# A recurrence and a gated feed-forward block on one core: second weight loads tied to other rows, and a new late order

## Chip, cores and metric

The kernel runs on one core of one Trainium2 chip. The metric is device time in microseconds (us) of the whole program, as the median of several runs. Engines: PE is TensorE, DVE VectorE, ACT ScalarE, POOL GpSimd, SP SyncE (which here only issues transfers). PEld is the weight load of TensorE, listed apart from its matmuls.

## What is computed

Inputs r, k, v, w have the shape (batch 4, heads 8, time 768, 48), u is (8, 48), all float32. The feed-forward weights are w_in (384 x 1024), conv_w (3 x 1024) and w_out (1024 x 384). They arrive as float64, which the kernel reads as pairs of 32-bit words. Cut to its core:

```python
for t in range(S):                       # per batch and head, state is 48 x 48
    cur = u * k[t] (outer) v[t]
    y[t] = r[t] @ (state + cur)
    state = w[t][:, None] * state + k[t] (outer) v[t]
x = y as (4, 768, 384)                   # the 8 heads side by side
h = relu(x @ w_in)                       # 384 -> 1024
conv = conv_w[0]*h[t-1] + conv_w[1]*h[t] + conv_w[2]*h[t+1]
out = (h * sigmoid(conv)) @ w_out        # 1024 -> 384
```

## The kernel before

**Tiling.** The 768 time steps of a batch are cut into 6 chunks of 128, so there are N = 24 chunks; chunk n works on all 8 heads at once. The feed-forward runs on 8 blocks of 384 time steps, two per batch. Blocks 6 and 7 are the last batch's. Chunk 21 is that batch's fourth chunk; block 6 needs its rows.

**A chunk.** `loads` (L653, SP) fetch w, k, r, v. PE turns them (L685), a scan on DVE makes the decay products in `kr`. Six small transfers on SP (`spread`, L728, 16 partitions each) bring pieces of `kr` into `last`, so that all heads stand where the matmuls want them. PE then makes the scores of the chunk, `half` (L843 on `kr` and `last`, and `fresh`, L853, on v and `kh`, a copy of k turned back by L752), and for the chunk before it `output`: L811 carries the old state in, L821 adds what comes from within the chunk. DVE makes the new state: `sa` (L886), `s` (L893), `sd` (L779), and ACT adds one part of `sd` from `last` (L782). An `output` lies in two PSUM banks. ACT copies its high half into xT (L903) and DVE the rest (L905). Six more small transfers on SP (L914) spread the heads that did not fit. After that xT holds the rows x of the feed-forward.

**A block.** Per feature slice of 128 (8 of them) PE makes 9 products x @ w_in (L925: three parts of 128 rows, times three for the high and low halves). The gating of a slice is a chain: relu (ACT L937), scale (ACT L938), two sums (DVE L939, L941), sigmoid (ACT L943), product (DVE L944), cast (ACT L946) and rest (POOL L947). Three products x w_out per slice and 128 time steps (L954) add up in one bank per 128 time steps. The sum is copied into `wide` (ACT L993) and sent (SP L994); the last block's banks are copied half on DVE (L988), half on ACT (L987) and sent from ACT's queue (L990).

**Word checks.** The weights were turned from float64 at the start. Whether all words were in the range that this way of reading them covers is checked late: `again(k)`, k = 0 to 5, loads the raw words a second time from ACT's queue (L640). The first three loads are a third of w_in, 1 MB each; the next two are three transfers of 384 KB of w_out, the last is two of them. Each goes into a slot of the ring `gh`, which it shares with the gated results. Two ACT passes per load (L570) add what is out of range into `flags`; PE sums the flags (L1108), and at the end a branch takes the program `general` if a flag is set. It isn't here.

**What sets the order.** Nothing of the order is written out by hand. Each step is given to a planner, `Plan`, with its reads, its writes and a rank. The planner simulates the engines with fixed lengths and takes the ready step with the lowest rank. The rank is the chunk's or block's own plus SHIFT[stage], SHIFT[kind] and FINE["stage.op"], which are tables of numbers; the stages are l, a, b (loads and two halves of a chunk), i, o (in- and out-products of a block), q (the second loads) and k. What comes out is one list per engine, which that engine goes through in order. On the chip a step waits only for the data and the buffers that it uses, and for what stands ahead of it in its engine's list. So a read that is given to the planner alone, such as the reads of `again`'s loads, puts the load behind something in the list, but makes no wait by itself.

**Transfers.** All transfers of SP and ACT take eight completion semaphores in turn, DMAHW0 to DMAHW7, in the order in which the program is built. An issue waits until the transfer that had this turn before it has landed.

Of the kernel before, what the change touches and what calls it, by code (L numbers as in the profile page):

```python
# [52 lines left out]
    a1=486, a10=10, a11=-18, a12=1721, a13=-81, a14=373, a15=1550, a16=-5, a17=-3444, a18=228, a19=55, a2=-187,  # L53
    a20=-277, a21=143, a22=-588, a23=-345, a3=564, a4=-460, a5=2857, a6=-907, a7=26, a8=-1139, adg=2121, adsel=469,
    afill=-1128, agather=278, aguard=-10, akback=101, akh=236, akt=-56, aones=259, ascan=8, asmall=202, aspread=80,
    atop=1, atr=6061, az=192, azh=-1916, b0=293, b1=54, b10=172, b11=311, b12=-289, b13=205, b14=-397, b16=-43,
    b17=-811, b18=422, b19=19, b2=8, b20=-700, b21=-277, b22=-4, b23=-23, b24=557, b3=-36, b4=114, b5=-77, b6=179,
    b8=-463, b9=123, bcph=2596, bcross=123, bhalf=477, boutput=378, bs=3878, bsa=-378, bsd=-16, bsdl=365, bsmall=10,
    bspread=-21, bxhih=-35, bxloh=-4306, c=-10, cexp=97, cfill=-99, cissue=-266, clo=239, ctr=191, cwords=-316,
    cwstt=-125, cwts=-21, i0=-310, i2=438, i3=-28, i5=-794, i6=-2808, i7=147, icast=-1967, igate=-1561, imm3=3579,  # L60
    imul=-1362, irelu=285, isig=-154, istt=1127, k=302, kissue=225, ksmall=-331, l0=-133, l1=55, l11=147, l12=-694,
    l13=-381, l14=143, l16=-1142, l17=-179, l18=361, l19=-27, l2=-167, l20=1421, l21=35, l22=-499, l23=-90, l3=-175,
    l4=-219, l5=-37, l7=19, l8=-366, l9=146, lload=5054, o0=-231, o1=195, o2=-305, o3=135, o4=-155, o5=-163, o6=966,
    o7=186, oissue=-72, omm3=8366, oout=-13, p0=-400, p1=-1988, p10=-778, p11=-1950, p12=-115, p13=-232, p14=-285,
    p15=589, p16=-556, p2=16, p3=-496, p4=5592, p5=162, p6=315, p7=29, p9=125, pcast=963, pexp=-965, plo=-954,
    pwstt=1024, pwts=1129, q0=1176, q2=-364, q3=1730, q4=-120, q5=166, qissue=-174, qwords=273, w1=-800, w2=105,
# [339 lines left out]
def rwkv_conv_moe_kernel(  # L406
# [13 lines left out]
    B, H, S, D = r.shape  # L420
# [9 lines left out]
    KT = DM // P  # L430
# [196 lines left out]
    def again(k):  # L627
# [10 lines left out]
        def fetch():  # L638
            for a, c in parts:
                nc.scalar.dma_start(out=a(), in_=c)  # L640
        op("ACT", "issue" if k < KT else "sends", fetch, [chunks[N - 1][x] for x in "wkrv"] + [("flag", N + 2 * k - 1)] * (k >= 1), [(raw, 0)],
           [raw], moves=(0.0027 * n, 309.0 if k < KT else 122.0, 8))
        small_words(words, raw, k, n, [(raw, 0)])

# [503 lines left out]
```

## Time and profile before

| | |
|---|---|
| time, median of 3 runs | 341.63 us (341.41 to 343.01) |
| the profiled execution | 342.61 us; its span in the trace 340.9 us; mean granted clock of TensorE 0.97 |
| busy of the span | PE 93%, PEld 87%, DVE 77%, ACT 65%, POOL 54% |
| moved | 41.36 MB, 121 GB/s in the mean |

A row of the timeline or the chain starts with its start in us from the start of the span and its length; brackets at its end give how long the engine stood idle before it and what ended that. ACTq and SPq are the engines' transfer issues. A row of windows lists, per stretch, the busy time of PE, PEld, DVE, ACT and POOL with the number of instructions, then the granted clock (1.00 is full), the mean busy share of the 16 DMA engines, and GB/s. A row of groups has busy us and mean ns of one, then the idle time ahead.

### The profile page before, as it was taken

To read this page: it belongs to the slowest core of one execution; us is meant where nothing else is said; L and a number is where in the kernel's file an instruction comes from. 1 tells how busy PE (TensorE), PEld (TensorE's weight loads), DVE (VectorE), ACT (ScalarE), POOL (GpSimd) and SP (SyncE) were. 2 spreads that over 40 slices of the span, in tenths; PEclk is the share of its full clock that TensorE was granted. 3 is DMA by queue.
4 is the path that set the end of the run, shared out by engine and by line. 5 is a ranking of instruction groups with operands and counts; after the bars stand their busy time and mean duration, and the time that the engine had idled before them with its cause. 6 is when DMAs were issued, how large, how long until landed. Compare 5 with 4: busy or idle time off the path is not lost.

```text
span 340.9 us, 11483 instructions
## 1 busy us (share of the span) xinstructions
PE 315.7 (93%) x4510; PEld 295.6 (87%) x4510; DVE 264.0 (77%) x623; ACT 222.9 (65%) x587; POOL 184.3 (54%) x242
## 2 busy tenths in 40 slices
PE   7858858789999999999999999999999989999993
PEld 3746647689999999989999999999999979999993
DVE  5899978899999798699887976899997526575340
ACT  4266435896886752578876534787954758898760
POOL 8978974898584862156862731438543501343140
PEclk9989995799999999999999999999999999999998
DMA  8997764661552374268152634564416445304212
GB/s 164 326 344 144 209 167 94 127 120 38 107 120 58 87 144 101 46 136 176 34 128 64 135 65 100 115 138 105 106 27 173 139 105 171 138 23 163 92 47 77
DMA packets 114546, 41.36 MB, mean 121 GB/s; under 512 B 103197, under 2 KB 110902, under 8 KB 113718
## 3 DMA queue, kind: packets, MB, share of 16 engines
q1 hardware_dynamic: 112036, 30.55, 40.6%
q10 hardware_dynamic: 2018, 6.88, 6.1%
q0 software_dynamic: 432, 3.15, 2.3%
q8 instruction: 36, 0.59, 0.7%
q14 instruction: 24, 0.20, 0.2%
HBM read 31.48 MB, written 4.72 MB: 106 GB/s over the span
## 4 chain that ended last, share of the span: by engine, by line
PE 73%; DMA 8%; DVE 7%; POOL 6%; issue 2%; ACT 2%; SPq 1%; POOLq 0%; DVEq 0%; ACTq 0%
PE bank L925 30%; PE bank L954 27%; PE bank L685 5%; PE bank L811 3%; DMA gh<-in_moe_w_in_dram,limits 3%; PE bank L821 2%; PE bank L843 2%; DMA last<-kr 2%; DMA gh<-in_moe_w_out_dram 2%; PE bank L853 2%; PE bank L752 2%; DMA k<-in_k_dram 1%; DVE wide L561 1%; POOL wo L579 1%; DVE kr L694 1%
## 5 line engine op out<-in xcount | busy, mean ns | idle before, releaser
L947 POOL TENSOR_TENSOR gh<-g,gh 128x384 fp32r<-128x384 f32 x64 | 64.8, 1020 | 98.5 <-ACT gh L946 97.2
L954 PE MATMUL bank<-wo,gh 128*128 128x384 f32 x576 | 117.5, 345 | 0.0
L925 PE MATMUL bank<-xT,wi 128*128 128x386 f32 x576 | 112.1, 347 | 1.5 <-issue 0.7
L925 PEld LDWEIGHTS bank<-xT,wi 128*128 128x128 f32 x576 | 104.0, 193 | 2.6 <-DVE dA L699 1.1
L954 PEld LDWEIGHTS bank<-wo,gh 128*128 128x128 f32 x576 | 98.8, 188 | 0.8
L939 DVE SCALAR_TENSOR_TENSOR a<-bank,cw,a 128x384 f32<-128x384 f32 x64 | 39.0, 611 | 19.0 <-ACT a L938 18.5
L937 ACT ACTIVATE bank<-bank 128x386 f32<-128x386 f32 x64 | 30.6, 478 | 22.1 <-PE bank L925 20.8
L944 DVE TENSOR_TENSOR g<-bank,a 128x384 f32<-128x384 f32 x64 | 35.1, 550 | 12.7 <-POOL gh L947 7.7
L744 POOL TENSOR_SCALAR_AFFINE_SELECT pm<-dg 64x512 f32<-64x512 f32 x46 | 30.2, 657 | 19.1 <-PE bank L821 14.0
L941 DVE SCALAR_TENSOR_TENSOR a<-bank,cw,a 128x384 f32<-128x384 f32 x64 | 38.9, 609 | 1.4 <-DVE a L939 0.4
L938 ACT ACTIVATE a<-bank,cw 128x384 f32<-128x384 f32 x64 | 37.0, 580 | 4.2 <-DVE g L944 2.4
L946 ACT CAST gh<-g 128x384 fp32r<-128x384 f32 x64 | 32.1, 510 | 10.5 <-DVE g L944 8.2
L943 ACT ACTIVATE a<-a 128x384 f32<-128x384 f32 x64 | 33.5, 523 | 5.7 <-DVE a L941 5.1
L732 POOL TENSOR_TENSOR z<-r,k 128x384 f32<-128x384 f32 x24 | 24.3, 1012 | 14.9 <-DVE dg L735 8.4
L694 DVE TENSOR_TENSOR_SCAN kr<-bank,one_end 128x387 f32<-128x387 f32 x24 | 22.9, 954 | 4.7 <-POOL kr L516 2.7
L903 ACT CAST xT<-bank 112x256 fp32r<-112x256 f32 x48 | 16.0, 377 | 14.4 <-PE bank L821 14.3
L734 POOL TENSOR_TENSOR z<-z,ubc 128x384 f32<-128x384 f32 x24 | 24.3, 1012 | 1.1
L811 PE MATMUL bank<-kr,sa 48*64 48x64 f32 (+1 forms) x288 | 21.0, 231 | 2.7 <-DVE bank L868 1.1
L702 DVE TENSOR_TENSOR_SCAN kr<-bank,dA 128x387 f32<-128x387 f32 x24 | 22.9, 952 | 0.1
L811 PEld LDWEIGHTS bank<-kr,sa 48*64 48x64 f32 (+1 forms) x288 | 14.6, 128 | 8.4 <-issue 3.1
L564 POOL TENSOR_TENSOR wide<-wide,wide 128x384 int32<-128x384 int32 (+2 forms) x18 | 16.7, 930 | 7.7 <-DVE wide L561 6.5
L905 DVE TENSOR_TENSOR xT<-bank,xT 112x256 fp32r<-112x256 f32 x48 | 18.2, 412 | 3.1 <-ACT xT L903 2.9
(108 smaller groups left out, 547.8 us busy)
## 6 DMA issues: line engine op xcount, KB each, us to landing
w<-in_w_dram SPq DMA_DIRECT2D x24, 192.0 KB, 3.9
k<-in_k_dram SPq DMA_DIRECT2D x24, 192.0 KB, 3.0
r<-in_r_dram SPq DMA_DIRECT2D x24, 192.0 KB, 3.4
v<-in_v_dram SPq DMA_DIRECT2D x24, 192.0 KB, 3.4
out_dram<-wide SPq DMA_DIRECT2D x21, 192.0 KB, 2.8
gh<-in_moe_w_in_dram ACTq DMA_DIRECT2D x3, 1024.0 KB
gh<-in_moe_w_out_dram ACTq DMA_DIRECT2D x8, 384.0 KB, 3.8
gh<-in_moe_w_out_dram SPq DMA_DIRECT2D x2, 1152.0 KB, 10.0
```

The lines of the kernel that those rows point to most:

```text
L744: op("POOL", "zh", lambda p=slice(HL * j, HL * (j + 1)): nc.gpsimd.affine_select(out=pm.t[p].rearrange("p g m t -> p (g m) t"), in_=dg.t[p ...
L811: nc.tensor.matmul(to(h, m, c, w), lhsT=q["sa" if h else "sd"].t[p, m, 0:w], rhs=rt(out_of, m)[p, HL * h:HL * (h + 1)], start=first(h, c), ...
L925: nc.tensor.matmul(t.t[:, 0:HB + 2], lhsT=wi[:, m, a, f * P:(f + 1) * P], rhs=xT[:, x0 + m, c, xs], start=(m == 0 and j == 0), stop=(m == ...
L937: ("ACT", "relu", lambda: nc.scalar.activation(out=h(0, width + 2), in_=h(0, width + 2), func=AF.Relu), [t], [t]),
L938: ("ACT", "mul", lambda: nc.scalar.mul(out=a(), in_=h(1), mul=cw[:, 1, bass.ds(f, 1)]), [t, "cw"], [a1]),
L939: ("DVE", "stt", lambda: nc.vector.scalar_tensor_tensor(out=a(), in0=h(0), scalar=cw[:, 0, bass.ds(f, 1)], in1=a(), op0=ALU.mult, op1=ALU. ...
L941: ("DVE", "stt", lambda: nc.vector.scalar_tensor_tensor(out=a(), in0=h(2), scalar=cw[:, 2, bass.ds(f, 1)], in1=a(), op0=ALU.mult, op1=ALU. ...
L943: ("ACT", "sig", lambda: nc.scalar.activation(out=a(), in_=a(), func=AF.Sigmoid), [], [a1]),
L944: ("DVE", "gate", lambda: nc.vector.tensor_tensor(out=g.t[:, 0:width], in0=h(1), in1=a(), op=ALU.mult), [t, a1], [g]),
L946: ("ACT", "cast", lambda: nc.scalar.copy(out=part(0)[:, 0:width], in_=g.t[:, 0:width]), [g], [key]),
L947: ("POOL", "lo", lambda: nc.gpsimd.tensor_tensor(out=part(1)[:, 0:width], in0=g.t[:, 0:width], in1=part(0)[:, 0:width].bitcast(F32), op=AL ...
L954: nc.tensor.matmul(acc.t[:, 0:DM], lhsT=part(a)[:, tt * P:(tt + 1) * P], rhs=wo[:, f, c, :], start=(f == 0 and a + c == 0), stop=(f == FT ...
```

## The change

`again` names other reads for the second loads: the x rows of the last batch's fourth chunk (chunk 21) in place of the last chunk's four loads, and, from the third load on, the check two loads back in place of the one before, so that two loads may be under way. The tables SHIFT and FINE have new numbers for the stages from about chunk 17 and block 4 on. Two lines of the tables are shown. Lines of the kernel after stand 3 higher from there on (L640 is L643).

```diff
...
 SHIFT = dict(
...
-    cwstt=-125, cwts=-21, i0=-310, i2=438, i3=-28, i5=-794, i6=-2808, i7=147, icast=-1967, igate=-1561, imm3=3579,
-    imul=-1362, irelu=285, isig=-154, istt=1127, k=302, kissue=225, ksmall=-331, l0=-133, l1=55, l11=147, l12=-694,
...
+    cwstt=-125, cwts=-21, i0=-310, i2=438, i3=-28, i5=-837, i6=-2830, i7=147, icast=-1967, igate=-1561, imm3=3579,
+    imul=-1362, irelu=285, isig=-154, istt=1127, k=295, kissue=225, ksmall=-331, l0=-133, l1=55, l11=147, l12=-694,
...
         def fetch():
             for a, c in parts:
                 nc.scalar.dma_start(out=a(), in_=c)
-        op("ACT", "issue" if k < KT else "sends", fetch, [chunks[N - 1][x] for x in "wkrv"] + [("flag", N + 2 * k - 1)] * (k >= 1), [(raw, 0)],
+        op("ACT", "issue" if k < KT else "sends", fetch, [("x", (B - 1) % 2, 3, j) for j in range(10)] + [("flag", N + 2 * k - 3)] * (k >= 2), [(raw, 0)],
            [raw], moves=(0.0027 * n, 309.0 if k < KT else 122.0, 8))
...
```

Up to about 210 us into the span the engines' lists are the same. Behind that they are another order of the same instructions. Three places:

**The second loads, on ACT.** In the rows below, gh_4039, gh_4215 and gh_4369 are the first three loads before, and gh_4249 and gh_4255 the first two after; xT casts are the copies of an `output` (of chunk 21: bank0 and bank6 before, bank6 and bank4 after). Before:

```order
L570 ACTIVATE gh_4039,flags_127<-gh_4039,limits_111 128x1024 [waits DMAHW4_49]
L946 CAST gh_4100<-g1_187 128x384 [waits DVE_49]
L782 ACTIVATE sd0_175<-s0_183,last1_159 112x48 [waits DMAHW3_49,DMAHW6_49,DMAHW2_49,DMAHW7_49,DMAHW1_49,DMAHW0_49]
L570 ACTIVATE gh_4039,flags_127<-gh_4039,limits_111 128x1024 [waits Activation_49]
L903 CAST xT_129<-bank0_64 112x4x64 [waits DVE_49,PE_49]
L903 CAST xT_129<-bank6_70 112x4x64 [waits PE_49]
L640 DMA gh_4215<-in_moe_w_in_dram 128x2048 [waits Pool_49]
L993 COPY wide3_137<-bank4_68 128x384 [waits PE_49]
L782 ACTIVATE sd1_176<-s0_183,last2_160 112x48 [waits DMAHW5_49,DMAHW4_49,DMAHW6_49,DMAHW2_49,DMAHW7_49,DMAHW0_49,DVE_49]
```

After:

```order
L906 CAST xT_129<-bank6_70 112x4x64 [waits PE_49]
L906 CAST xT_129<-bank4_68 112x4x64 [waits PE_49]
L758 COPY kh1_172<-bank7_71 128x2x48 [waits PE_49]
L757 COPY kh1_172<-bank7_71 128x336
L949 CAST gh_4131<-g1_187 128x384 [waits DVE_49]
L996 COPY wide3_137<-bank3_67 128x384 [waits PE_49]
L643 DMA gh_4249<-in_moe_w_in_dram 128x2048 [waits DMAHW0_49,Pool_49]
L643 DMA gh_4255<-in_moe_w_in_dram 128x2048 [waits DMAHW2_49,Pool_49]
L996 COPY wide0_134<-bank2_66 128x384 [waits PE_49]
L940 ACTIVATE bank7_71<-bank7_71 128x386 [waits PE_49,Activation_49]
```

Before, the first load was issued ahead of these rows, its two passes stood around chunk 21's `output`, and the second load came right behind the copies of that `output`. After, the first two loads stand side by side, behind a copy of bank3, and no pass of a check has run by then.

**The small transfers, on SP.** At the same place: `last2` belongs to chunk 23 (the last one), the xT rows are the x rows of chunk 21 and those ahead of it, `wide` is an output. Before, six rows of `last` (one output between them) and six of x:

```order
L728 DMA last2_160<-kr2_154 16x2x130 [waits DMAHW2_49,DVE_49]
L994 DMA out_0_dram<-wide1_135 128x384 [waits DMAHW3_49,Activation_49]
L728 DMA last2_160<-kr2_154 16x2x130 [waits DMAHW4_49]
...
L728 DMA last2_160<-kr2_154 16x2x130 [waits DMAHW0_49]
L914 DMA xT_129<-xT_129 16x2x512 [waits DMAHW2_49,DVE_49]
...
L914 DMA xT_129<-xT_129 16x2x512 [waits DMAHW7_49]
L994 DMA out_0_dram<-wide3_137 128x384 [waits DMAHW0_49,Activation_49]
```

After:

```order
L917 DMA xT_129<-xT_129 16x2x512 [waits DMAHW2_49,DVE_49]
L917 DMA xT_129<-xT_129 16x2x512 [waits DMAHW3_49]
...
L917 DMA xT_129<-xT_129 16x2x512 [waits DMAHW7_49]
L997 DMA out_0_dram<-wide3_137 128x384 [waits DMAHW1_49,Activation_49]
L731 DMA last2_160<-kr2_154 16x2x130 [waits DMAHW3_49,DVE_49]
...
L731 DMA last2_160<-kr2_154 16x2x130 [waits DMAHW7_49]
L731 DMA last2_160<-kr2_154 16x2x130 [waits DMAHW0_49]
```

The x pieces now go ahead of the pieces of `last`, not behind them. Turn 0, for which the sixth piece of `last` waits, was taken last by the first second load (gh_4249 above), and turns 3 to 7 by x pieces.

**The copies of chunk 21's `output`, on DVE.** Before:

```order
L893 TENSOR_TENSOR s0_183<-bank3_67,sa0_179 112x192 [waits DVE_49]
L779 TENSOR_TENSOR sd1_176<-s0_183,kr2_154 112x3x48 [waits DVE_49,PE_49]
L905 TENSOR_TENSOR xT_129<-bank0_64,xT_129 112x4x64 [waits Activation_49]
L905 TENSOR_TENSOR xT_129<-bank6_70,xT_129 112x4x64 [waits Activation_49]
L868 MEMSET bank5_69 1x1 [waits PE_49]
```

After:

```order
L908 TENSOR_TENSOR xT_129<-bank6_70,xT_129 112x4x64 [waits Activation_49]
L908 TENSOR_TENSOR xT_129<-bank4_68,xT_129 112x4x64 [waits Activation_49]
L947 TENSOR_TENSOR g1_187<-bank0_64,a11_185 128x384 [waits Pool_49]
L709 TENSOR_TENSOR kr2_154<-bank1_65,kr2_154 128x3x128 [waits PE_49]
L896 TENSOR_TENSOR s0_183<-bank5_69,sa0_179 112x192 [waits DVE_49]
L782 TENSOR_TENSOR sd1_176<-s0_183,kr2_154 112x3x48 [waits DVE_49]
```

The state `s` and `sd` stood ahead of the x rows and stand behind them now.

**PE behind chunk 21's `output`, and at its end.** After that `output`, PE made 24 out-products (L954), the `output` of chunk 22 begins (L811), and all of chunk 23's scores followed. Block 6's in-products came behind all of it. After the change (L957 are out-products, L928 in-products of block 6, L814 begins the `output` of chunk 22):

```order
L688 MATMUL bank1_65<-ident_86,r1_143 128x128 x3
L755 MATMUL bank7_71<-ident_86,kr2_154 128x128 x3
L957 MATMUL bank3_67<-wo_133,gh_3716 128x384 x9
L957 MATMUL bank3_67<-wo_133,gh_4059 128x384 x9
L957 MATMUL bank3_67<-wo_133,gh_4131 128x384 x6
L957 MATMUL bank2_66<-wo_133,gh_3716 128x384 x9
L957 MATMUL bank2_66<-wo_133,gh_4059 128x384 x9
L957 MATMUL bank2_66<-wo_133,gh_4131 128x384 x6
L957 MATMUL bank6_70<-wo_133,gh_3716 128x384 x3
L928 MATMUL bank7_71<-xT_129,wi_132 128x386 x9
L928 MATMUL bank4_68<-xT_129,wi_132 128x386 x9
L928 MATMUL bank0_64<-xT_129,wi_132 128x386 x9
```

Three feature slices of block 6 are now ahead of chunk 23's scores; six out-products of block 5 follow them. The last rows of PE before, and after:

```order
L1108 MATMUL bank0_64<-ones_f_91,fsum_193 1x1
L954 MATMUL bank2_66<-wo_133,gh_4779 128x384 x3
L954 MATMUL bank6_70<-wo_133,gh_4624 128x384 x9
L954 MATMUL bank6_70<-wo_133,gh_4749 128x384 x9
L954 MATMUL bank6_70<-wo_133,gh_4779 128x384 x6
```

```order
L1111 MATMUL bank0_64<-ones_f_91,fsum_193 1x1
L957 MATMUL bank7_71<-wo_133,gh_4730 128x384 x3
L957 MATMUL bank7_71<-wo_133,gh_4811 128x384 x3
L957 MATMUL bank4_68<-wo_133,gh_4811 128x384 x3
L957 MATMUL bank6_70<-wo_133,gh_4811 128x384 x3
L957 MATMUL bank7_71<-wo_133,gh_4811 128x384 x3
```

Before, one bank's 24 products stood last; after, the three banks of the last 384 time steps end one behind the other, three products each.

## Rows read from the trace of the kernel before

**Rows 1.** The page's parts 1 and 2: busy us, and tenths in 40 slices.

```profile
PE 315.7 (93%) x4510; PEld 295.6 (87%) x4510; DVE 264.0 (77%) x623; ACT 222.9 (65%) x587; POOL 184.3 (54%) x242
PE   7858858789999999999999999999999989999993
```

**Rows 2.** Busy times by stretches of 20 us (columns in the section above).

```profile
260.00:280.00 20.00, 18.79 (x396) 17.29 (x395) 10.01 (x27) 11.57 (x26) 6.33 (x7) 1.00 0.54 164
...
300.00:320.00 20.00, 20.00 (x115) 20.00 (x114) 13.43 (x24) 18.21 (x38) 5.86 (x6) 1.00 0.20 70
```

**Rows 3.** PE's timeline behind chunk 21's `output`.

```profile
268.93 4.50 PE L954 MATMUL bank<-wo,gh 128*128 128x384 f32 x24
273.37 0.27 PE L811 MATMUL bank<-kr,sa 48*64 48x64 f32 x1
...
274.00 0.28 PE L843 MATMUL bank<-last 48*64 48x64 f32 x2
275.48 0.28 PE L843 MATMUL bank<-last 48*64 48x64 f32 x3 [1.21 <-DMA last<-kr]
```

**Rows 4.** The chain that ended last, in 254 to 281 us: start, length, what.

```profile
258.50 0.33 PE bank L752 x3
...
268.95 6.49 DMA last<-kr
```

**Rows 5.** Line L728, all 120 transfers: from the issue's end to landing.

```profile
DMA to landing us min/median/max: 1.8/1.9/5.9
```

**Rows 6.** ACT's timeline, the second loads.

```profile
269.11 0.34 ACTq L640 DMA_DIRECT2D gh<-in_moe_w_in_dram  x1
...
280.41 0.48 ACT L993 COPY wide<-bank 128x384 f32<-128x384 f32 x1 [0.18 <-PE bank L954]
280.42 0.33 ACTq L640 DMA_DIRECT2D gh<-in_moe_w_in_dram  x1
```

**Rows 7.** Busy times by stretches of 1 us, during the second load.

```profile
272.00:273.00 1.00, 1.00 (x8) 1.00 (x7) 0.00 (x0) 0.00 (x0) 0.00 (x0) 1.00 0.99 410
...
274.00:275.00 1.00, 0.28 (x15) 0.14 (x6) 0.01 (x1) 0.00 (x0) 0.00 (x0) 1.00 0.48 74
```

**Rows 8.** Line L728, the one transfer issued at 260.0 us.

```profile
DMA to landing us min/median/max: 5.0/5.0/5.0
```

**Rows 9.** The chain that ended last, from 280 us on.

```profile
280.38 7.97 PE bank L925 x45
...
317.52 13.25 PE bank L954 x75
...
330.88 4.89 PE bank L954 x27
```

**Rows 10.** The timeline of all engines at the end.

```profile
335.80 0.36 DVE L988 COPY wide<-bank 128x192 f32<-128x192 f32 x1 [3.81 <-PE bank L954]
336.19 0.32 ACT L987 COPY wide<-bank 128x192 f32<-128x192 f32 x1 [3.85 <-DVE wide L988]
336.54 0.34 ACTq L990 DMA_DIRECT2D out_dram<-wide  x1
```

**Rows 11.** Line L990: the output issued at 332.37, then that at 336.54.

```profile
DMA to landing us min/median/max: 2.6/2.6/2.6
...
DMA to landing us min/median/max: 2.7/2.7/2.7
```

**Rows 12.** SP's timeline, the x pieces of chunk 21.

```profile
271.32 4.88 SPq L914 DMA_DIRECT2D xT<-xT  x6
```

**Rows 13.** DVE's timeline behind chunk 21's `output`.

```profile
270.15 0.48 DVE L779 TENSOR_TENSOR sd<-s,kr 112x144 f32<-112x144 f32 x1 [0.46 <-DVE s L893]
```

**Rows 14.** Line L914, all 48 transfers of x pieces.

```profile
DMA to landing us min/median/max: 2.0/3.1/4.3
```

**Rows 15.** Groups on ACT, 280 to 341 us: the word checks.

```profile
L570 ACT ACTIVATE gh<-gh,limits 128x1024 f32<-128x1024 int32 (+5 forms) x9 | 11.1, 1233 | 0.0
```

**Rows 16.** The page's part 3, ACT's queue: packets, MB, share of 16 engines.

```profile
q10 hardware_dynamic: 2018, 6.88, 6.1%
```

More of the change, by code (lines that the diff above doesn't have):

```diff
@@ L52 @@
 SHIFT = dict(
-    a1=486, a10=10, a11=-18, a12=1721, a13=-81, a14=373, a15=1550, a16=-5, a17=-3444, a18=228, a19=55, a2=-187,
-    a20=-277, a21=143, a22=-588, a23=-345, a3=564, a4=-460, a5=2857, a6=-907, a7=26, a8=-1139, adg=2121, adsel=469,
+    a1=486, a10=10, a11=-18, a12=1721, a13=-81, a14=373, a15=1550, a16=-5, a17=-3423, a18=252, a19=36, a2=-187,
+    a20=-275, a21=1135, a22=-766, a23=-617, a3=564, a4=-460, a5=2857, a6=-907, a7=26, a8=-1139, adg=2121, adsel=469,
     afill=-1128, agather=278, aguard=-10, akback=101, akh=236, akt=-56, aones=259, ascan=8, asmall=202, aspread=80,
@@ L56 @@
     atop=1, atr=6061, az=192, azh=-1916, b0=293, b1=54, b10=172, b11=311, b12=-289, b13=205, b14=-397, b16=-43,
-    b17=-811, b18=422, b19=19, b2=8, b20=-700, b21=-277, b22=-4, b23=-23, b24=557, b3=-36, b4=114, b5=-77, b6=179,
+    b17=-964, b18=452, b19=-70, b2=8, b20=-395, b21=-277, b22=-239, b23=-49, b24=539, b3=-36, b4=114, b5=-77, b6=179,
     b8=-463, b9=123, bcph=2596, bcross=123, bhalf=477, boutput=378, bs=3878, bsa=-378, bsd=-16, bsdl=365, bsmall=10,
     bspread=-21, bxhih=-35, bxloh=-4306, c=-10, cexp=97, cfill=-99, cissue=-266, clo=239, ctr=191, cwords=-316,
-    cwstt=-125, cwts=-21, i0=-310, i2=438, i3=-28, i5=-794, i6=-2808, i7=147, icast=-1967, igate=-1561, imm3=3579,
@@ L61 @@
-    imul=-1362, irelu=285, isig=-154, istt=1127, k=302, kissue=225, ksmall=-331, l0=-133, l1=55, l11=147, l12=-694,
-    l13=-381, l14=143, l16=-1142, l17=-179, l18=361, l19=-27, l2=-167, l20=1421, l21=35, l22=-499, l23=-90, l3=-175,
-    l4=-219, l5=-37, l7=19, l8=-366, l9=146, lload=5054, o0=-231, o1=195, o2=-305, o3=135, o4=-155, o5=-163, o6=966,
-    o7=186, oissue=-72, omm3=8366, oout=-13, p0=-400, p1=-1988, p10=-778, p11=-1950, p12=-115, p13=-232, p14=-285,
+    cwstt=-125, cwts=-21, i0=-310, i2=438, i3=-28, i5=-837, i6=-2830, i7=147, icast=-1967, igate=-1561, imm3=3579,
@@ L65 @@
+    imul=-1362, irelu=285, isig=-154, istt=1127, k=295, kissue=225, ksmall=-331, l0=-133, l1=55, l11=147, l12=-694,
+    l13=-381, l14=143, l16=-1337, l17=506, l18=411, l19=-29, l2=-167, l20=1140, l21=-171, l22=-649, l23=125, l3=-175,
+    l4=-219, l5=-37, l7=19, l8=-366, l9=146, lload=5054, o0=-231, o1=195, o2=-305, o3=135, o4=-382, o5=-916, o6=906,
+    o7=62, oissue=-72, omm3=8366, oout=-13, p0=-400, p1=-1988, p10=-778, p11=-1950, p12=-115, p13=-232, p14=-285,
     p15=589, p16=-556, p2=16, p3=-496, p4=5592, p5=162, p6=315, p7=29, p9=125, pcast=963, pexp=-965, plo=-954,
-    pwstt=1024, pwts=1129, q0=1176, q2=-364, q3=1730, q4=-120, q5=166, qissue=-174, qwords=273, w1=-800, w2=105,
+    pwstt=1024, pwts=1129, q0=1177, q1=77, q2=-829, q3=1580, q4=-63, q5=182, qissue=-174, qwords=273, w1=-800, w2=105,
```

69 rows, old and new, of the table FINE are left out of this document.

## The prediction

> **What bounds the kernel now.** I read the page first: TensorE (PE) is busy 93% of the span and is the only engine that shows nines from the first quarter to the end [rows 1]. It isn't full before 80 us, where the diff moves nothing; behind that the busy times by stretches show one hole, 260 to 280 us, where it lacks 1.2 of 20 us [rows 2]. The PE timeline shows this as one wait: the scores of the last chunk (L843, chunk 23) stop for 1.21 us until a piece of `last` has landed [rows 3]. The chain of waits gives the piece: begun at 268.95, landed 6.49 us later, 5.9 of them behind the issue itself (0.6) [rows 4], where the median of such pieces is 1.9 us [rows 5]. What lies beside it is the second load of the first third of w_in, 1 MB on ACT's queue, issued at 269.11 [rows 6]; the DMA engines then run at 410 GB/s and are quiet in the stretch from 274 [rows 7]. A piece issued at 260.0, beside the load before, took 5.0 us [rows 8]. So a small transfer that meets such a load lands about 1 us after the load's data. From 280.4 us on PE runs without a gap worth naming to its last product [rows 9]; then come a copy on DVE, one on ACT and an output DMA [rows 10], which lands 2.7 us after its issue [rows 11].
>
> **Part 1, the wait moved.** In the planner the second loads now come behind the rows of chunk 21. The built program says something narrower. The first load waits on no x row: its semaphores are DMAHW0 (the transfer that last had this turn, v of chunk 23) and Pool. It is held by its place in ACT's queue, behind the copy of bank3. That bank is full after two transposes and 24 output products behind chunk 21's `output`. Call the end of that `output` D (in the trace of before about 269.0, where the products behind it begin [rows 3]). A transposition costs 0.33 us [rows 4], a product 13.25/75 = 0.177 us [rows 9], so the load issues at D + 0.66 + 4.24 = D + 4.9; a load behind such a copy is issued within 0.01 us of the copy's start [rows 6]. The second load waits for turn 2, the first x piece, and follows at once. Price of the issues on ACT: 0.33 us each [rows 6], beside running instructions, so nothing. What is queued behind them there is a copy of bank2 (needed from D + 9.2) and the relu of block 6, which waits for PE anyway.
>
> The x pieces: in the trace of before, SP begins the first at D + 2.3 and needs 4.88 us for six [rows 12]: the last issue ends at D + 7.2. There DVE made `s` and `sd` ahead of the low halves of the x rows, `sd` for 0.48 us behind a wait of 0.46 [rows 13]; now both stand behind them, which gives back about 0.8: D + 6.4, and with six issues of 0.6 us, none long, D + 5.1. At the median landing of 3.1 us [rows 14] the rows are there at D + 8.2 to 9.5, at the longest (4.3) by D + 10.7. PE wants them after 51 products: D + 0.66 + 9.0 = D + 9.7. I take no wait; the bounds are 0 and 1.0 us. In before PE asked for them only after everything of chunk 23, so this margin is new.
>
> The pieces of `last` for chunk 23 now leave behind the x pieces: five need the turns 3 to 7 (x pieces) back, the sixth needs turn 0, which is the first load. By the trace that load takes from 269.11 to about 274.3, 5.2 us [rows 6, 7]: D + 10.1. The sixth is out 0.6 us later and lands in 1.9 us, D + 12.6; if the second load (1 MB at 400 GB/s, 2.6 us more, quiet at D + 12.7) holds it as the 268.95 piece was held, at about D + 13.9. PE needs it after 27 products of block 6 at 7.97/45 = 0.177 us (4.8) and 6 of block 5 (1.1), and 0.6 us into the scores (274.00 less 273.37 in the trace) [rows 3, 9]: D + 16.2. So 2.3 to 3.6 us are to spare, where before there was a lack of 1.21. **Term: -1.2 us.** Nothing follows it at once: behind it PE's work is the same products in another order.
>
> **Part 2, the word checks go later.** The same twelve passes run (nine behind 280 take 11.1 us, 1.23 each [rows 15]); in before three ran ahead of that, now all run after D + 16. Their 3 x 1.23 = 3.7 us fall where ACT was busy 18.2 of 20 us [rows 2]. But block 6's first three gatings now start 27 products earlier, before the last chunk and not after it, and leave that room: about 2 us of ACT each at the page's durations. The last gating decides: after the last in-product PE now has 23 groups of three out-products (12.2 us), of which the last three need the last gating. In before 102 products stood there (75 and 27 [rows 9]), 18 us. The chain relu, scale, two sums, sigmoid, gate, cast and rest costs about 5.5 us with nothing between, with the ten other ACT instructions there about 8; 10.6 us are there. I take 0; if the backlog is 3 us larger PE waits 0.4. PE's product on the flags (L1108) waits for the last check, stood 24 to 27 products before the end and now stands 15; but that check comes ahead of the last cast on ACT, so it is no later bound than the gating.
>
> **Part 3, the end.** Before, one bank's products stood last, 24 in a row, and one output was left. Now the three banks end 0.53 us apart. Each needs 0.36 us on DVE and then 0.32 on ACT, with 0.03 between [rows 10], so the copies keep up with PE: the last DMA leaves 0.82 us after PE's end, in before 0.77. But it leaves 0.37 us behind another one, where before it was alone. Of an earlier pair 0.83 us apart the second took 2.6 us, the lone one 2.7 [rows 11]. Bounds 0 and 0.7 us, I take **+0.2**.
>
> **Other late shifts** reorder the products and chunk work from 210 us on. PE had no wait there and the instructions are the same ones. Bounds: -0.1, and +0.5 for a wait of its own; I take 0.
>
> **Sum.** -1.2 + 0.2 = -1.0 against the profiled execution (342.61 us, span 340.9): 341.6. That execution is 0.98 us over the median of the runs, and no row tells whether some of this is the very stall. So the median should lose between 0.2 and 1.0; I take 0.8: **340.8 us**.
>
> **Rivals.** *The stall comes back at the same place (18%).* The two loads may share the engines and land together, at D + 12.7. The sixth piece then leaves at D + 13.3, and lands in 1.9 us at D + 15.2 or, with 5.0 us as beside a load [rows 8], at D + 18.3: PE waits up to 2.1, say 1.2, and the time is 342.0. For it: the order puts both issues side by side. Against it: one queue's descriptors come in turn.
>
> *Slower: the x rows meet the loads (16% in two sizes).* The last x piece leaves between D + 4.5 and D + 6.4, the loads at D + 4.9 and D + 5.3. The piece of 268.95 left 0.16 us ahead of a load and was caught. Caught behind the first load, x lands 1.1 us after D + 10.1, D + 11.2, and PE waits 1.5: 342.3. Caught behind both, at D + 12.7 + 1.1 = D + 13.8, PE waits 4.1: 344.9. From a wait of 2.5 us on it is slower than before by more than 0.5%. Against it: the x pieces of before left inside a load's flight, too, and none of the 48 took over 4.3 us [rows 14]. I give 7% to the small size, 9% to the large.
>
> [...] ACT's queue moved 6.88 MB in 2018 packets [rows 16], 3.4 KB each. [...]
>
> *No gain (10%).* The stall was in the profiled execution alone: 341.6 stays, with +0.2 for the end, 341.8.
>
> *It does not hold the loads at all* is no case of its own: the first load is in truth not held by the rows, and the sum above counts it at its place in ACT's queue.
>
> **How the numbers follow.** The forecast has 51%, and its own range is 340.3 to 341.4. A gain over 0.5% (1.7 us; about what a measurement of this kernel tells from no change) would need more than the whole stall: 5%. Slower by over 0.5% is the large size of the second rival: 9%. Within 0.5%: 86%. The range from 340.1 to 342.6 takes in the forecast, the returned stall, no gain and the small size.
>
> **What would show it.** Right: no PE wait on `last` or on x after 210 us; the first two loads issued side by side about 5 us after chunk 21's `output`; PE's end about 1.2 us nearer to the start; the last output's issue 0.8 us behind it. Wrong: PE waiting at its first product of block 6 on xT (second rival), at L843's successor on `last` (first rival), or at the last out-products on POOL (part 2).

## The result and the profile after

The kernel after takes 344.47 us (343.98 to 345.3), the kernel before in the same comparison 342.0 (341.41 to 343.01): a ratio of 1.0071, interval 1.0051 to 1.0092. A second comparison (e10) gave 1.0051 (1.0032 to 1.0070). The change makes the kernel slower by about 2 us. The forecast was 340.8 us, and the range 340.1 to 342.6.

The profiled execution took 344.35 us, its span 342.5, at a granted clock of 0.956. The page's parts 1 and 2, beside [rows 1]:

```profile
PE 315.0 (92%) x4510; PEld 296.1 (86%) x4510; DVE 264.5 (77%) x623; ACT 221.3 (65%) x587; POOL 184.2 (54%) x242
PE   6758977789999999999999999999999999999991
```

PE is as busy as before. Behind the first quarter two slices differ: the 8 of 273 to 281 us, where PE waited before, is a 9, and the last slice has 1 where there was 3. To compare the two executions one needs a common point, since the part ahead of the change differs by chance. The last PE instructions ahead of the first difference in order are three transpositions of r, in the timeline of before and of after:

```profile
208.29 0.49 PE L685 MATMUL bank<-ident,r 128*128 128x128 f32 x3
```

```profile
207.53 0.49 PE L688 MATMUL bank<-ident,r 128*128 128x128 f32 x3
```

So after was 0.76 us ahead where the lists were still the same. From here on PE's products took 127.48 us before (to 335.77) and 127.60 after (to 335.13): no gain. The waits of PE behind 200 us in after (engine and line, the one waited for, us in total, times, longest) have one row:

```profile
PE bank L814 <- DVE bank L871: 1.1, 1, 1.1
```

The wait of 1.21 us on `last` [rows 3] is gone, and one of 1.1 us stands in its place: the second half of chunk 22's carried products (the first half ran at 280.65) waits until DVE has written one element, a mark, into their bank. The expectations call this place `carried`. Rows of the chain of waits of after (start, length, what) tell why:

```profile
265.14 0.48 PE bank L688 x3
265.62 0.33 PE bank L755 x3
265.95 4.21 PE bank L957 x24
...
270.24 5.45 DMA gh<-in_moe_w_in_dram
...
275.71 5.35 DMA last<-kr
...
281.08 0.02 ACT sd L785
...
281.32 0.48 ACT bank L940
...
281.83 0.59 ACT a L941
...
282.44 0.62 DVE a L942
283.06 0.06 DVE bank L871
```

Read from below: DVE could not write the mark earlier, as the first sum of a gating stood ahead of it; that sum needed ACT's scale, that the relu; and the relu of block 6's third slice stood in ACT's list behind the sum from `last` (L785). At that sum ACT stood until a piece of `last` had landed at 281.06.

The other half is the end of the program. Rows behind the branch, of before and then of after (line, operation, count, ns min/median/max, first and last start); SP's eight take the transfers' semaphores:

```profile
L1116 SPq EVENT_SEMAPHORE  x8: 17/17/17, 335.1 to 339.2; - x8
...
L1116 DVEq COMPARE_BRANCH  x1: 72/72/72, 336.4 to 336.4; - x1
...
L1116 DVEq EVENT_SEMAPHORE  x1: 21/21/21, 339.4 to 339.4; - x1
...
L1143 DVEq DRAIN  x2: 10/14/17, 339.5 to 340.3; - x2
```

```profile
L1119 SPq EVENT_SEMAPHORE  x8: 17/17/17, 336.0 to 339.0; - x8
...
L1119 DVEq COMPARE_BRANCH  x1: 72/72/72, 335.8 to 335.8; - x1
...
L1119 DVEq EVENT_SEMAPHORE  x1: 21/21/21, 339.3 to 339.3; - x1
...
L1146 DVEq DRAIN  x2: 10/64/118, 341.6 to 342.0; - x2
```

DVE's first row behind the branch starts at 339.4 and 339.3. Before, DVE goes on 0.1 us later, after 2.3 us later, and in after all engines wait for it in a barrier. In before the barrier had waited for SP, which came to it at 340.0.

The expectations below take that row for DVE's wait for the last output. It isn't one. The semaphore that it names is raised by DVE alone, last at 336.2 and 335.5. It comes 2.9 to 4.0 us behind DVE's branch in every run, whether the outputs have landed or not: in e12 at 338.0, where SP sees the last output at 338.3, and in e4 (its rows follow) at 339.0, where the last output, issued at 333.54, landed 1.9 us later. So it is the first instruction at the place where the branch lands, and it comes late by itself. In before and after the last output happens to land 0.2 us ahead of it.

```profile
L1119 DVEq COMPARE_BRANCH  x1: 72/72/72, 334.9 to 334.9; - x1
...
L1119 DVEq EVENT_SEMAPHORE  x1: 21/21/21, 339.0 to 339.0; - x1
```

In the gap, from 339.3 to 341.6, the transfers of after show one packet alone, on the queue that the page calls `instruction` (packets, MB, share):

```profile
q14 instruction: 1, 0.01, 1.0%
```

Before has such a packet, too (at 340.0, 0.6 us behind the row), without a gap. What differs is their number from the first engine's branch on, seven in before and eight in after:

```profile
q14 instruction: 7, 0.06, 2.0%
```

```profile
q14 instruction: 8, 0.07, 1.8%
```

Counted in the same way, the runs with a gap at DVE's end (e3, e10 and e11 as well) have eight, and all others seven.

Measured from the common point, the time is thus made up: PE +0.12; from PE's end to SP's last row for an output 3.9 us after, 3.5 before, +0.4; from there to the end of the span 3.5 us after, 1.7 before, +1.8. Together 2.3 to 2.4 us, close to the 2.47 by which the medians differ.

### The profile page after: what moved, and what is told of

Same layout as the page of the kernel before. It is cut to its first block, busy times and chain, and to the rows that moved or that the text cites. A ratio compares the mean times of both kernels' runs of the same rounds, so it can differ in the third digit from the quotient of the medians.

```text
span 342.5 us, 11480 instructions
## 1 busy us (share of the span) xinstructions
PE 315.0 (92%) x4510; PEld 296.1 (86%) x4510; DVE 264.5 (77%) x623; ACT 221.3 (65%) x587; POOL 184.2 (54%) x242
## 4 chain that ended last, share of the span: by engine, by line
PE 74%; DMA 9%; DVE 9%; POOL 3%; issue 2%; ACT 1%; SPq 1%; POOLq 0%; DVEq 0%
PE bank L928 28%; PE bank L957 28%; PE bank L688 5%; PE bank L814 3%; PE bank L824 3%; DMA gh<-in_moe_w_in_dram,limits 3%; PE bank L846 2%; DMA last<-kr 2%; DMA r<-in_r_dram 2%; PE bank L856 2%; DMA gh<-in_moe_w_in_dram 2%; PE bank L755 2%; DVE kr L697 1%; DVE kr L705 1%; DVE xT L908 1%
## 5 line engine op out<-in xcount | busy, mean ns | idle before, releaser
L957 PE MATMUL bank<-wo,gh 128*128 128x384 f32 x576 | 116.3, 345 | 0.0
L928 PE MATMUL bank<-xT,wi 128*128 128x386 f32 x576 | 111.4, 346 | 0.7 <-DVE xT L908 0.7
L928 PEld LDWEIGHTS bank<-xT,wi 128*128 128x128 f32 x576 | 103.4, 192 | 1.7 <-DVE xT L908 0.9
L957 PEld LDWEIGHTS bank<-wo,gh 128*128 128x128 f32 x576 | 99.0, 188 | 0.7
L814 PE MATMUL bank<-kr,sa 48*48 48x64 f32 (+1 forms) x288 | 21.8, 238 | 3.9 <-DVE sa L893 1.8
L906 ACT CAST xT<-bank 112x256 fp32r<-112x256 f32 x48 | 16.2, 377 | 13.2 <-PE bank L824 13.0
L814 PEld LDWEIGHTS bank<-kr,sa 48*48 48x48 f32 (+1 forms) x288 | 15.3, 133 | 9.8 <-issue 3.9
L814 PE MATMUL bank<-kr,sd 48*48 48x64 f32 (+1 forms) x240 | 18.8, 239 | 2.6 <-DVE bank L871 2.6
```

The lines of the kernel that those rows point to most:

```text
L814: nc.tensor.matmul(to(h, m, c, w), lhsT=q["sa" if h else "sd"].t[p, m, 0:w], rhs=rt(out_of, m)[p, HL * h:HL * (h + 1)], start=first(h, c), ...
L928: nc.tensor.matmul(t.t[:, 0:HB + 2], lhsT=wi[:, m, a, f * P:(f + 1) * P], rhs=xT[:, x0 + m, c, xs], start=(m == 0 and j == 0), stop=(m == ...
L957: nc.tensor.matmul(acc.t[:, 0:DM], lhsT=part(a)[:, tt * P:(tt + 1) * P], rhs=wo[:, f, c, :], start=(f == 0 and a + c == 0), stop=(f == FT ...
```

## The experiments

Ratios are against the kernel before on the same chip, with 95% intervals.

| run | ratio |
|---|---|
| after, twice | 1.0071 (1.0051 to 1.0092), 1.0051 (1.0032 to 1.0070) |
| e1: after, 1 skipped DVE instruction more | 0.9985 (0.9955 to 1.0016) |
| e2: after, 2 more | 0.9991 (0.9970 to 1.0012) |
| e3: before, 123 more | 1.0065 (1.0039 to 1.0090) |
| e4: after, loads behind the pieces of `last` | 1.0061 (1.0035 to 1.0087) |
| e5: e4, the last check earlier | 0.9978 (0.9957 to 0.9999) |
| e6 and e12: after, second load behind the pieces, 6 more | 0.9968 (0.9946 to 0.9990), 0.9962 (0.9937 to 0.9986) |
| e7: before with the new reads | 1.0049 (1.0030 to 1.0068) |
| e8: after with the old reads | 1.0009 (0.9975 to 1.0044) |
| e9: e2, ACT's sum from `last` later | 0.9974 (0.9953 to 0.9994) |
| e11: e6 without the 6 | 0.9990 (0.9965 to 1.0015) |

### The end: where a block of DVE's code ends (e1, e2, e3, e11)

DVE executes 794 instructions before and 789 after. All that stands behind the branch moves by that. To move it without changing anything that runs, instructions were added to `general`, which the branch skips:

```diff
         nc.vector.memset(pick, 0.0)
+        nc.vector.memset(pick, 0.0)
```

once more (e1), twice more (e2), and 123 times more in the kernel before (e3).

> The kernel after with one more DVE instruction in the program for bad words (`general`), which is skipped: nothing executed changes, but DVE's code behind the branch stands one instruction (64 bytes) later. In the trace of after DVE's wait for the last output ends at 339.3 us and its next instruction starts 2.3 us later, with one 8192-byte transfer of the instruction queue between; DVE executed 789 instructions, in before 794, five fewer. Theory A (a block of DVE's code ends between those two instructions, and the next is fetched only then): with 1 more the block ends one instruction earlier, behind the wait and ahead of the branch; the gap stays, the time stays 344.5. Rival B (the end is longer for its three outputs or for another engine): 344.5 too.

> As the run before, but two more DVE instructions in the skipped program. Theory A: now the wait itself is the first instruction of the new block, which is fetched while DVE still waits for the output; the gap goes, time 342.4 (344.5 less 2.1). Rival B: no change, 344.5.

> The kernel before with 123 more DVE instructions in the skipped program: 128 (8192 bytes of 64) less the 5 by which after is shorter, so that the code behind the branch stands at the same place of a block as in after. Theory A: the gap of 2.1 to 2.3 us appears, 344.0. Rival B: no change, 342.0.

DVE's rows in e1, then in e3:

```profile
L1120 DVEq EVENT_SEMAPHORE  x1: 21/21/21, 340.2 to 340.2; - x1
...
L1147 DVEq DRAIN  x2: 10/14/17, 340.4 to 341.1; - x2
```

```profile
L1117 DVEq EVENT_SEMAPHORE  x1: 21/21/21, 340.7 to 340.7; - x1
...
L1144 DVEq DRAIN  x2: 10/64/118, 343.3 to 343.7; - x2
```

e2 and e3 came as theory A has it: the gap goes with two skipped instructions and comes into the kernel before with 123 (2.6 us, ratio 1.0065, with not one executed instruction changed). Rival B is out: three outputs at the end, or another engine, would not care for DVE's skipped code. e1 was a miss: one instruction was enough, where the gap was expected to stay.

The miss goes away if the row is read as above, as the place where the branch lands. Theory A had a branch between this row and the drain; the trace shows none, and before and e1 have 0.1 us between the two starts. If in after a block of code ends directly behind the row, DVE lands there late and needs the next block at once. With one more instruction (e1) the row is the first of the new block, and what follows comes with it. That what DVE lacks is the next block is argued: the trace doesn't name the engine of a packet. But it fits that the runs with a gap have one packet more, that in every run one starts 0.6 us (0.9 in e3) behind the row, and that DVE goes on 2.35 us behind the row in after, e10 and e11 (2.6 in e3).

e11 takes the version of e6 (below) without its six padding instructions:

> The kernel with the second load alone tied to the pieces, as before in this study but without the six more instructions in the skipped program: what is executed is the same, DVE's code behind the branch stands six instructions earlier, and by theory A the block's end then falls between DVE's first barrier instructions, two further on than in after. Theory A: a gap of 2.0 to 2.6 us between DVE's instructions behind the last output, of which the other engines' barrier hides about 0.6; ratio 1.002 to 1.004 where the version with the six has 0.997. Rival B (the gap of after had another cause): 0.997.

```profile
L1146 DVEq DRAIN  x2: 17/65/113, 337.8 to 340.0; - x2
...
L1146 DVEq EVENT_SEMAPHORE  x2: 21/21/21, 338.4 to 340.3; - x2
```

Here the first drain comes at once, at 337.8, and the gap of 1.6 us stands ahead of the second one (from 338.4 to 340.0): the block's end has moved on by two instructions, as the list that is two shorter asks. The gap is smaller than the 2.0 to 2.6 us expected: counted from the first row (337.7) the 2.35 us are the same, and the two instructions pass in them. The ratio of 0.9990 is under the 1.002 to 1.004 expected; against 0.9968 and 0.9962 it has the right sign, but the intervals overlap, so the size in time rests on the trace.

### The wait of 1.1 us: loads, pieces, or ACT's list (e4, e6, e9)

My first theory (C) took the sixth piece for the culprit, as it had to wait for the turn of the first load. e4 ties all second loads to the pieces, e6 only the second one, by the `* (k == 1)` of its edit below (with six skipped instructions more, which keep DVE clear of the block's end):

```diff
-        ... [("x", (B - 1) % 2, 3, j) for j in range(10)] + [("flag", N + 2 * k - 3)] * (k >= 2), [(raw, 0)],
+        ... [("x", (B - 1) % 2, 3, j) for j in range(10)] + [("flag", N + 2 * k - 3)] * (k >= 2) + lasts(N - 1) * (k == 1), [(raw, 0)],
```

> The kernel after with the second loads tied to the pieces of `last` of chunk 23 as well: in the order the first load now comes behind a later place on ACT, the sixth piece of `last` no longer waits for the load's turn, and the second load is issued behind a piece of `last` that has landed. DVE's code stands three instructions further than in after, clear of the block's end by theory A. Theory C (the 1.1 us that PE waits at 282 us in after come from ACT, which stands at the sum from `last` until the sixth piece has landed, and that piece had to wait until the first load had landed): no wait over 0.3 us of PE behind 210 us, and with the gap at the end gone as well 344.5 - 1.1 - 2.1 = 341.3. Rival D (the loads and the pieces share the DMA engines, the turn plays no part): PE still waits about 1 us there, 342.4.

> The kernel after with the second load alone (of six) tied to the pieces of `last`; the first stays at its place, issued about 5.1 us behind the end of chunk 21's `output`. One transfer fewer then stands between, so that the six pieces wait for the turns of the six x pieces and none for the first load. (Six more DVE instructions in the skipped program keep DVE's code clear of a block's end.) Theory C (turn): all six pieces leave without a break although the first load is in flight, the sixth about 2 us earlier than in after (measured from the `output`: D + 8.5 rather than D + 10.6); ACT's sum from `last` waits under 0.3 us, PE's wait of 1.1 us at `carried` is gone, about 341.6 where before has 342.8. Theory D (sharing of the DMA engines): the pieces leave early but land only about 1 us behind the first load (D + 11.5), which is early enough as well: the same time, but landings of 3 us and more. If the wait stays, the turn isn't its cause.

> The version with the second load alone tied to the pieces, and the six instructions, timed again in more rounds: theory C and A together, ratio 0.997, between 0.995 and 0.999.

In both the wait is gone, though e4 missed its time by 3 us, for a reason told below; e6 and its repeat e12 make the kernel faster than before. But the landings show that the reason was wrong. In after SP issued the six pieces from 271.14 on (the fifth at 273.91); the landings of the first and the fifth, which this view counts from the issue's start:

```profile
271.14 5.15 SPq L731 DMA_DIRECT2D last<-kr  x6
```

```profile
DMA to landing us min/median/max: 8.9/8.9/8.9
...
DMA to landing us min/median/max: 7.0/7.0/7.0
```

The first landed at 271.14 + 8.9 = 280.0, 1.0 us before the sixth (281.06). All six were late, and five of them waited for no load's turn. What held them shows in the packets by queue (q10 is ACT's, q1 SP's), from 272.0 to 274.5 and from 274.5 to 278.0:

```profile
q10 hardware_dynamic: 98, 0.80, 79.6%
```

```profile
q10 hardware_dynamic: 162, 1.14, 79.0%
q1 hardware_dynamic: 208, 0.22, 17.7%
```

For 2.5 us SP's queue moved no packet while the first load ran; then both moved side by side, with the output that stood ahead of the pieces first. In e6, with one load in flight, the pieces landed faster, but not fast (load, third relu and sum on ACT, then the landings of the six):

```profile
271.13 0.37 ACTq L649 DMA_DIRECT2D gh<-in_moe_w_in_dram  x1
...
280.58 0.48 ACT L946 ACTIVATE bank<-bank 128x386 f32<-128x386 f32 x1
280.97 0.33 ACT L791 ACTIVATE sd<-s,last 112x48 f32<-112x48 f32 x1
```

```profile
DMA to landing us min/median/max: 4.5/5.3/6.5
```

In e6's list, however, the third relu stands ahead of the sum from `last`, so e6 changes two things. To tell the pieces from the list, e9 left the loads and the pieces as they are in e2 and put only that sum behind the third scale (what comes later on ACT shifts a little with it):

```diff
            [old, *lasts(n)], [(sd, 1)], [sd, last])
+        if n == N - 1:
+            plan.ops[-1][3].add([i for i, t in enumerate(plan.tags) if t[0] == "i6" and plan.what[i] == "mul"][2])
```

> The kernel after with two more DVE instructions in the skipped program (no gap at the end), and one thing moved: ACT's sum from `last` of chunk 23 is given to the planner behind the scale of block 6's third slice. In after that sum stands ahead of the third relu, and ACT stands at it until the pieces of `last` have landed at 281.06 us; nothing of the loads or the pieces is changed. Theory Q (the 1.1 us that PE waits come from what is queued behind the sum on ACT): the relu runs 1.5 us earlier, PE's wait of 1.1 us at `carried` is under 0.3, and the time is 1.1 us under that of the run with two instructions (ratio 0.999): 0.996. Rival P (the pieces are simply late for PE too): PE waits about 1 us at the scores or `carried` of chunk 23 all the same, ratio 0.999.

```profile
270.42 0.91 ACTq L645 DMA_DIRECT2D gh<-in_moe_w_in_dram  x2
...
279.86 0.48 ACT L944 ACTIVATE bank<-bank 128x386 f32<-128x386 f32 x1
...
282.18 0.32 ACT L787 ACTIVATE sd<-s,last 112x48 f32<-112x48 f32 x1
```

Both loads still leave side by side (0.91 us for two), the pieces land until 281.1 as in after, the relu runs at 279.86 instead of 281.32, and the waits view has no row for PE behind 206 us: theory Q. From the common point PE takes 126.6 us in e9 and 127.2 in e2, where its wait is 0.9. The ratio of 0.9974 against 0.9991 of e2 has the right sign, but the two intervals overlap. The pieces were late in after, but PE itself could have lived with them; ACT's list could not.

### The checks, if they come last (e4, e5, e7, e8)

e4 lost the wait and was still slow. Its profiled execution has these two waits near the end, the first of PE, the second of SP:

```profile
PE bank L1111 <- DVE fsum L1109: 1.5, 1, 1.5
```

```profile
SPq L1119 <- SPq L1119: 3.8, 1, 3.8
```

The last check's two passes stood behind ACT's copies of the last outputs, so the product on the flags came last on PE, and the engines took the branch only at 335 us. SP then had its next instruction 3.8 us after it had jumped over `general`, at 339.0, and DVE's came at the same time, though the last output had landed at 335.4. e5 moved the sixth load and its check ahead by the table alone:

```diff
-    "q3.sends": 650, "q3.words": 273, "q4.sends": -270, "q4.words": 907, "q5.sends": 189, "q5.words": -426,
+    "q3.sends": 650, "q3.words": 273, "q4.sends": -270, "q4.words": 907, "q5.sends": -2000, "q5.words": -3000,
```

> As the run with the loads tied to the pieces of `last`, with the sixth second load and its check put earlier by numbers of the table (q5.words -3000, q5.sends -2000): in the order the two last passes now stand ahead of ACT's copies of the last outputs, and PE's product on the flags 6 out-products ahead of the end. In that run PE waited 1.5 us for the flags at its end, the outputs were issued behind the checks, and all engines read the result of the checks only then. Theory C (the wait on the pieces is gone, only the checks were late there): no wait of PE over 0.3 us behind 210 us, the branch read ahead of the last output, and 1.1 us less than after clear of the code gap: 341.6 where before has 342.8 on this chip. Rival D (the lateness of the checks stays, at another place): 344.3 as that run.

Ratio 0.9978 where e4 has 1.0061: the late checks cost 0.8%, nearly 3 us. Two more runs split the change. e7 has the tables of before and the new reads, e8 the new tables and the old reads:

```diff
-        ... [chunks[N - 1][x] for x in "wkrv"] + [("flag", N + 2 * k - 1)] * (k >= 1), [(raw, 0)],
+        ... [("x", (B - 1) % 2, 3, j) for j in range(10)] + [("flag", N + 2 * k - 3)] * (k >= 2), [(raw, 0)],
```

> The kernel before with its own tables, and the change's reads of the second loads alone. In the order both first loads now come behind the copies of chunk 22's `output`, later than the pieces of `last`, and PE's product on the flags stands last. Theory C: the wait of 1.21 us on `last` is gone; but the checks start later, and the flags come last: PE waits there, and the branch is read 1 to 3 us later; together 342.0 to 344.5 where before has 342.8. Rival D: the wait on `last` stays, 342.8 or more. Rival E: the change of reads is free, 341.6.

> The kernel after with the reads of the second loads as in before, the new tables kept (DVE's code clear of a block's end by two instructions). The first load goes before chunk 21's `output` again, one load at a time. Theory C: the sixth piece of `last` waits for the turn of the second load, which is issued behind the first check; that check's end decides, PE waits 0 to 2 us there; 341.6 to 344 where before has 342.8. Rival D: no wait there, since one load at a time shares the engines less: 341.6.

In both, PE has no wait over 0.3 us behind 206 us, so the wait on `last` is gone with either half. e7 gives it back at the end as e4 does: the flags come last, and SP's row is the same:

```profile
SPq L1116 <- SPq L1116: 3.8, 1, 3.8
```

e8's PE is 0.95 us faster than before from the common point (207.73 to 334.26), but its branch, too, is taken later than in before (SP's at 334.6, before 332.4), the last output lands 4.2 us behind PE's end where before has 3.5, and DVE's first row behind the branch comes 4.9 us behind it where before has 3.6. It comes out even (1.0009; the interval reaches from 0.9975 to 1.0044). Neither half of the change alone makes the kernel slower by the gap that the whole has: both have DVE's code clear of the block's end.

e10 is the kernel after once more:

> The kernel after once more, beside the others on one chip. By the theories so far: ratio 1.007, gap at the end 2.3 us, wait at `carried` 1.1 us.

It has the same gap (DVE's first row behind the branch at 339.9, the next at 342.2) and a wait of 1.0 us at the same place.

## Why the prediction was wrong, point by point

**What failed first: a price that was not in the sum at all.** Part 3 ended with the landing of the last output and put all that stands behind it at nothing, without a reason: no step asked where DVE's code behind the branch lies. The change shortens DVE's list by five instructions, and this, by theory A, puts a block's end directly behind the place where the branch lands. That is 2.3 us, of which SP's own way to the barrier hides about 0.5: +1.8. e1, e2 and e3 show that the gap comes and goes with the place of DVE's code alone, whatever the change is about; with the block's end out of the way the kernel after has a ratio of 0.9985 and 0.9991, which is no change. The trace of before could not show the gap, but the length of DVE's list could be compared. That code comes in blocks fits two measurements: the packets of q14 from the branch on are 8192 bytes each, and e3 moved DVE's code by 128 instructions against after (123 and the 5) and got the gap back (2.6 us, in after 2.3). The 64 bytes per instruction of the expectations are 8192 over these 128, if a packet is a block; the page's 0.79 MB on both instruction queues are 69 for each of the 11480 instructions that ran. Both are estimates.

**Part 1, "2.3 to 3.6 us are to spare. Term: -1.2 us."** The wait on `last` went, as forecast, but the term measured +0.12 with the rest of PE's work. Two steps failed. The first is the landing: the load's issue (270.24, D + 5.1 with D = 265.14), the two loads side by side, the end of the first (D + 10.5) and the sixth piece's issue (D + 10.6) came as told, to half a microsecond; the pieces landed at D + 15.9 where I took D + 12.6 to 13.9. The upper figure held the piece until about 1 us behind the second load, and in after it landed 0.8 us behind it; but this load, taken as quiet at D + 12.7, landed at 270.70 + 9.5 = 280.2, D + 15.1 (the landing of the second load, from its issue's start):

```profile
DMA to landing us min/median/max: 9.5/9.5/9.5
```

The forecast also reckoned with neither the output ahead of the pieces on SP's queue nor the 2.5 us in which this queue stood still. And it read [rows 5] as counted from the issue's end; it counts from the start, so that the lower figure has the 0.6 us of the issue twice, and the slow piece of before is 6.49 us against 1.9. The second step is the need: I asked when PE wants the pieces (D + 16.2, which would have been just enough) and not who else does. ACT's sum from `last` stands in its list ahead of the third relu, and its wait stopped ACT from 279.58 to 281.08. What is queued behind a waiting instruction was asked for the load's issue, and not for this one. e9 shows that this alone made the new wait.

**The x rows** came in time: SP's sixth issue ended at 270.4, D + 5.2 (forecast D + 5.1 to 6.4), and PE began its products on them without a wait. The rival that they meet the loads did not happen.

**Part 2, the checks, 0:** right for after, where PE's product on the flags found them ready. e4, e5 and e7 show how near it was: with the checks a little later the price is up to nearly 3 us and comes at two places, at PE's product (e4) and at the jump, whose next code takes SP up to 3.8 us. I had only the first.

**Part 3, the end, +0.2 in bounds of 0 to 0.7:** measured +0.4 up to the last output's landing. The last output's issue ends 1.3 us behind PE's end (336.47 less 335.13; before 1.1), the rest is a landing that takes 0.2 us longer:

```profile
335.15 0.36 DVE L991 COPY wide<-bank 128x192 f32<-128x192 f32 x1 [0.17 <-PE bank L957]
335.29 0.58 ACT L990 COPY wide<-bank 128x192 f32<-128x192 f32 x2 [0.48 <-DVE wide L991]
335.64 0.83 ACTq L993 DMA_DIRECT2D out_dram<-wide  x2
```

Two outputs are issued in one go, as was told, and the second issue takes longer.

**Other late shifts, 0:** without their waits PE's products take 126.27 us before (127.48 less 1.21) and 126.49 after (127.60 less 1.11): +0.2, inside the bounds.

**The rivals.** The first one (the stall comes back at the same place, 342.0) had the late pieces, and nearly the size by luck. Its way did not happen: the loads did not land together but in turn, as its argument against had it (at 275.69 and 280.2, issued 0.46 us apart), and PE waited not on the pieces but on what ACT's wait had held up. The slower case that held 9% was the wrong mechanism; the gap at DVE's end was in no rival. The versions with neither the new wait nor the gap, e9 and e6, have 0.9974 and 0.9962 to 0.9968; the forecast of 340.8 is 0.9976 of 341.63, inside their intervals. They are other orders than after, so this supports the size of the gain that was forecast and doesn't prove it. The change as it is does not reach it.

## What to carry to other kernels

When a change moves work past a wait, ask for every engine that waits for the late thing, and what stands behind that wait in its list; the engine with the visible stall need not be the one that stalls next. In a kernel with a branch at its end, compare the length of each engine's list before and after as well: here five fewer on DVE came with a gap of 2.3 us behind the place where the branch lands, and one or two skipped instructions more took it away (e1, e2). e6 is the version to keep here: 0.9962 to 0.9968 of before.

## What the hardware showed that was not expected

DVE and SP had their next instruction late behind the jump over `general`: DVE's came 2.9 to 4.0 us behind its branch in all runs, SP's 2.5 to 3.8 us. POOL's came 0.4 us behind its branch in before (332.1 to 332.5). Mostly the last outputs hid this (SP's 2.6 us in after); in e4 and e7, with 3.8 us and the branch taken late, it came last.

In after, e3 and e10, where by theory A a block of code ends directly behind the place where the jump lands, DVE lost 2.3 to 2.6 us more. With one skipped instruction more (e1) it lost nothing (340.2, then 340.4), with the end two instructions further along (e11) 1.6 us.

Transfers of 16 KB behind two loads of 1 MB on another queue landed 7.0 to 8.9 us after the start of their issue (five of six; the sixth, issued later, 5.35), where 1.9 is the usual [rows 5]; SP's queue stood still for 2.5 us ahead of that. From 274.5 to 278.0 us packets of both queues moved side by side (208 of SP's queue, 162 of ACT's); in the 2.5 us ahead of that no packet of SP's queue moved, although an output issued at 270.7 stood there. Why its first packets came so late stays open.
